# Two pairs of VectorE sums merged into one each, with negative copies from ScalarE

## The chip, the cores and the metric

The kernel runs on one core of a Trainium2 chip. The metric is the device time of one execution in microseconds, the median of several runs. Engines are called as in the profile: PE (TensorE, with PEld for its weight loads), DVE (VectorE), ACT (ScalarE), POOL (GpSimd), SP (SyncE, which issues most DMAs here).

## What is computed

The reference has three stages, all on 2 series of 12480 tokens with 128 channels:

```
u      = x * v
h      = (relu(pos_emb @ w1) @ w2) * exp(-0.01 * pos)
y      = irfft(rfft(u, 2S) * rfft(h, 2S))[:S]        # a long causal convolution, per channel
t      = x * y                                        # 24960 tokens x 128
t      = (g * cos(g)) @ w_out,   g = t @ w_in         # d_ff = 2048
out    = (g * min(max(g+3,0),6) / 6) @ w_out2,  g = t @ w_in2
```

## The kernel before

The convolution is done in place of a longer FFT as a product of two cyclic transforms on a grid of 111 x 113 points (12543 points), with a sign pattern `sig` for the second (odd) half. Channels go in groups of two (`CH = 2`, `NG = 64` groups), each with both series. One group passes four stages, which different rounds of one loop work on: `s1` (first transform along 111, on PE, 4 products in a group of columns `g`: 0 and 1 for the two series, 2 for the filter), `s2h` and `s2u` (second transform along 113 of the filter `xh` and of the signal `xp`), then on DVE `mk_pq` and `mk_y` (product of the spectra), `s2i` (back along 113), `s1i` (back along 111, giving `v1` and `v2` in PSUM), and `mk_w` (DVE), `fin` (POOL) and `store` (SP).

The loop `for i in range(NG)` at line 536 is written out by hand, in program order for every engine: in round `i` it issues, in this order, the loads for group i+3, the stores of group i-4, `s1(i+1, 2)`, `s2i(i-2, 0)`, `s1(i+1, 0)`, `s2i(i-2, 1)`, `s1(i+1, 1)`, `make_p(i+2)`, in odd rounds `copy_h`, `make_q`, `sums_h`, `s2h(i)`, `mk_w(i-3)`, one step of the two weight decoders (`step_decode`, lines 114 to 139: some rounds have three ACT instructions of it, some none), `make_u(i+2)`, `fin(i-3)`, `s2u(i)`, `s1i(i-2)`, `mk_pq(i)`, `mk_y(i)`. Each engine takes its own instructions in that order, so an instruction that waits holds all behind it on its engine.

What PE writes goes to PSUM, and is brought to SBUF by ACT: `at` (line 298, from `ap`), `b` (line 470, from `bp`), `hs` (line 422, from `xh`), `v2s` (line 480, from `v2`). PSUM buffers: `ps_a` has two, which `s1(.,2)`, `s2i(.,0)`, `s2i(.,1)` and `s1(.,1)` take in turn; `ps_c` has one, for `s1(.,0)` and `s2h`; `ps_v` one, for `v1` and `v2` in two banks. A PSUM buffer is free again when its last reader is through.

The product of the spectra: `xp` holds real and imaginary part of the signal (z = 0, 1), `hs` those of the filter. `mk_pq` makes `p = xp * hs_re` in SBUF and then overwrites `xp` (in PSUM) with `q = xp * hs_im`; both are 896 elements wide. `mk_y` writes `y_re = p_re - q_im` and `y_im = p_im + q_re`, two instructions of 448 elements. `mk_w` writes `w = v1 + v2` and `w = v1 - v2` into the two halves of each row, two instructions of 456 elements:

```
for z, op in ((0, ALU.subtract), (1, ALU.add)):             # mk_y, line 451
    nc.vector.tensor_tensor(out=y[..z half..], in0=p[:, z], in1=q[:, 1 - z], op=op)
for h, op in ((0, ALU.add), (M2, ALU.subtract)):            # mk_w, line 485
    nc.vector.tensor_tensor(out=o[:, :, h:h + M2], in0=v1_t[i], in1=v2_t[i], op=op)
```

After the loop (lines 572 to 635) the last groups are finished in halves by series; those use `mk_pq` and `mk_y` with a series number `b`, but their own `w_of` in place of `mk_w`. A DMA at line 619 reads back from `scr` the first 448 tokens of all earlier groups (it can only start when their stores have landed), `pass_on` sends the last groups' ones straight to `x0`, and `split_x(0)` (line 671: `x0h` on ACT, `x0l` on DVE) opens the two expert stages, `moe_phase`, which take the rest of the time.

Of the kernel before, what the change touches and what calls it, by code (L numbers as in the profile page):

```python
# [9 lines left out]
FP32 = mybir.dt.float32  # L10
# [3 lines left out]
ACTF = mybir.ActivationFunctionType  # L14
ALU = mybir.AluOpType
# [6 lines left out]
B, S, D = 2, 12480, 128  # L22
R = 64
N1, N2 = 111, 113
N = N1 * N2
NP1 = 112
K1 = 56
M2 = 57
# [21 lines left out]
def kernel(  # L50
# [19 lines left out]
    nc = tc.nc  # L70
# [90 lines left out]
    def conv_phase(cctx):  # L161
# [30 lines left out]
        p_2 = cctx.enter_context(tc.tile_pool(name="p_2", bufs=2))  # L192
# [5 lines left out]
        x_t, v_t, a_t, hs_t, xp_t, pq_t, y_t, b_t, v1_t, v2_t, w_t, wa_t, z_t = ({} for _ in range(13))  # L198
# [82 lines left out]
        def mm(out, lhsT, rhs, rhs2=None):  # L281
            m = lhsT.shape[-1]
            nc.tensor.matmul(out=out[:OD], lhsT=lhsT[:, :OD], rhs=rhs)  # L283
            nc.tensor.matmul(out=out[OD:m], lhsT=lhsT[:, OD:m], rhs=rhs if rhs2 is None else rhs2)  # L284
# [123 lines left out]
        p_1 = cctx.enter_context(tc.tile_pool(name="p_1", bufs=1))  # L408
# [5 lines left out]
        def s2_mm(o, q0, q1, a):  # L414
            for z in range(2):
                mm(o[z], cs[:, z, :], a[:, z, q0:q1, :])

        def s2h(i):
            ap = ps_c.tile([N2, 2, 4, K1], FP32, tag="a", name="xh")
            s2_mm((ap[:, 0], ap[:, 1]), 8, 12, a_t[i])  # L420
            hs = p_2.tile([N2, 2, 4 * K1], FP32, tag="hs", name="hs")
            nc.scalar.copy(hs, ap.rearrange("p z s k -> p z (s k)"))
            hs_t[i] = hs

        def s2u(i):
# [5 lines left out]
        def mk_pq(i, b=None):  # L431
            if i not in pq_t:
                xv = xp_t.pop(i)[:, :, :448].rearrange("p z (b k) -> p z b k", b=B)
                pq_t[i] = (p_1.tile([N2, 2, B, 4 * K1], FP32, tag="pq", name="pq"), xv)
            p, xv = pq_t[i]
            hs = hs_t[i]
            for z, o in ((0, p), (1, xv)):
                if b is None:
                    h = hs[:, z, :].unsqueeze(1).unsqueeze(1).to_broadcast([N2, 2, B, 4 * K1])
                    nc.vector.tensor_tensor(out=o, in0=xv, in1=h, op=ALU.mult)  # L440
                else:
                    h = hs[:, z, :].unsqueeze(1).to_broadcast([N2, 2, 4 * K1])
                    nc.vector.tensor_tensor(out=o[:, :, b], in0=xv[:, :, b], in1=h, op=ALU.mult)

        def mk_y(i, b=None):
            p, q = pq_t[i]
            if i not in y_t:
                y_t[i] = p_2.tile([N2, 8, 2 * K1], FP32, tag="y", name="y")
            bs = slice(0, B) if b is None else slice(b, b + 1)
            y = y_t[i][:, 4 * bs.start:4 * bs.stop]  # L450
            for z, op in ((0, ALU.subtract), (1, ALU.add)):
                nc.vector.tensor_tensor(
                    out=y[:, :, z * K1:(z + 1) * K1],
                    in0=p[:, z, bs].rearrange("p b (s k) -> p (b s) k", k=K1),
                    in1=q[:, 1 - z, bs].rearrange("p b (s k) -> p (b s) k", k=K1), op=op,
                )

        def s2i(i, g, pool=None):
            if not 0 <= i < NG:
# [12 lines left out]
        def s1i(i):  # L472
            b = b_t.pop(i)
            v = ps_v.tile([NP1, 2, 512], FP32, tag="v", name="v")
            v1, v2 = [v[:, z, :8 * M2].rearrange("p (a b) -> p a b", b=M2) for z in range(2)]
            for z, o in ((1, v2), (0, v1)):
                mm(o, gm[:, z, :], b[:, :, z * M2:(z + 1) * M2])
            v1_t[i] = v1
            v2_t[i] = p_1.tile([NP1, 8, M2], FP32, tag="v2s", name="v2s")
            nc.scalar.copy(v2_t[i], v2)  # L480

        def mk_w(i):
            w = w_t[i] = p_2.tile([NP1, B, 2, CH, MP], FP32, tag="w", name="w")
            o = w.rearrange("p b s c n -> p (b s c) n")
            for h, op in ((0, ALU.add), (M2, ALU.subtract)):
                nc.vector.tensor_tensor(out=o[:, :, h:h + M2], in0=v1_t[i], in1=v2_t[i], op=op)

        def fin(i):
            z = z_t[i] = p_2.tile([NP1, B, CH, MP], FP32, tag="z", name="z")
# [46 lines left out]
        for i in range(NG):  # L536
# [15 lines left out]
            if i:  # L552
                make_q(i + 2)
            sums_h((i + 3) // 2, (1,) if i and i % 2 == 0 else (0,))
            s2h(i)
            if i >= 3:
                mk_w(i - 3)
# [9 lines left out]
            if i >= 2:  # L567
                s1i(i - 2)
            mk_pq(i)
            mk_y(i)  # L570

        n = NG
# [29 lines left out]
        s1i_3(0)  # L602
        s2i(n - 2, 0)
        mk_pq(n - 1, 0)
        mk_y(n - 1, 0)
        s2i(n - 1, 0)
        s1i_of(n - 2, 0, ps_c, "a")
        s1i_of(n - 1, 0, ps_p, "p")
        w_of(n - 3, 0, w3[:, 0])
        fin_of(n - 3, 0, z3[:, 0], nc.gpsimd)  # L610
        mk_pq(n - 1, 1)
        mk_y(n - 1, 1)
        w_of(n - 2, 0, w2_[:, 0])
        fin_of(n - 2, 0, z2[:, 0], nc.gpsimd)
# [342 lines left out]
```

## Time and profile before

| | us |
|---|---|
| median of 3 runs (2617.3 to 2620.01) | 2617.63 |
| the profiled execution | 2617.47 |
| its span in the profile | 2615.7 |

| busy in the span | us | share | instructions |
|---|---|---|---|
| PE | 2598.3 | 99% | 16362 |
| DVE | 2344.5 | 90% | 3188 |
| ACT | 2150.5 | 82% | 3140 |
| POOL | 2394.7 | 92% | 1321 |

The filter is made in the first 38 us, the loop runs from about 38 to 520 us, the last groups are finished by about 535 us, and the expert stages fill the rest. Busy shares over the whole span mix these, so the loop is read by itself. In a timeline each row is one instruction (or several merged, xN), with its start and its length; two instructions in a row on one engine can overlap, so what an instruction costs its engine is the step from its start to the next one's start. Idle time and what ended it stand in square brackets.

### The profile page before, as it was taken

The numbers are of one execution on the slowest core, as the hardware profiler recorded it, in microseconds if no ns is written. First come the engines' busy times: TensorE is split into PE (matmuls) and PEld (weight loads), VectorE is DVE, ScalarE is ACT, GpSimd is POOL, SyncE is SP. The second block draws the span as 40 slices with busy tenths as digits, with TensorE's granted clock in tenths as the row PEclk, the third lists the DMA queues.
The fourth block names the chain that finished last, engine by engine and source line by source line (L and its number), as shares of the span: only waits on it lengthen the run. The fifth ranks groups of instructions, "written<-read, shape, count | busy, mean of one in ns | idle before, by whom it ended". The sixth has DMA issues, their size and how long they took to land.

```text
span 2615.7 us, 45720 instructions
## 1 busy us (share of the span) xinstructions
PE 2598.3 (99%) x16362; PEld 2149.6 (82%) x16362; DVE 2344.5 (90%) x3188; ACT 2150.5 (82%) x3140; POOL 2394.7 (92%) x1321
## 2 busy tenths in 40 slices
PE   9999999989999999999999999999999999999999
PEld 6777777768888888888888888888888888888888
DVE  7999998779999999999999999999999999999997
ACT  5666665588888888888888888888888888888885
POOL 6999999788999999999999999999999999999998
PEclk9999999999999999999999999999999999999999
DMA  4433433210000000000000000000000000000000
GB/s 120 108 102 100 104 105 83 67 33 8 17 9 17 9 17 9 17 9 17 17 9 17 9 17 9 17 9 17 9 16 17 9 17 9 17 9 17 9 9 13
DMA packets 88312, 79.86 MB, mean 31 GB/s; under 512 B 57028, under 2 KB 78870, under 8 KB 88086
## 3 DMA queue, kind: packets, MB, share of 16 engines
q1 hardware_dynamic: 87790, 76.80, 10.9%
q8 instruction: 132, 2.16, 0.3%
q14 instruction: 94, 0.77, 0.1%
q10 hardware_dynamic: 296, 0.13, 0.0%
HBM read 51.15 MB, written 25.74 MB: 29 GB/s over the span
## 4 chain that ended last, share of the span: by engine, by line
PE 97%; ACT 1%; POOL 1%; DVE 1%; DMA 1%; issue 0%; DVEq 0%; POOLq 0%; ACTq 0%; SPq 0%
PE acc L784 39%; PE hb L715 20%; PE ha L715 19%; PE ap L284 5%; PE v L284 4%; PE xp L284 3%; PE bp L284 3%; PE xh L284 2%; PE ap L283 1%; PE rp L336 1%; PE hps L349 0%; PE bp L283 0%; DMA x<-scr 0%; POOL lo L749 0%; ACT r L736 0%
## 5 line engine op out<-in xcount | busy, mean ns | idle before, releaser
L774 POOL TENSOR_TENSOR lo<-g,hi 128x1024 fp32r<-128x1024 f32 (+1 forms) x390 | 938.7, 2407 | 141.3 <-DVE hi L771 131.9
L749 POOL TENSOR_TENSOR lo<-g,hi 128x1024 fp32r<-128x1024 f32 (+1 forms) x392 | 941.2, 2401 | 2.4 <-ACT hi L744 1.9
L726 ACT ACTIVATE k<-ha,biasq 128x512 int32<-128x512 f32 (+1 forms) x768 | 494.6, 687 | 214.0 <-PE ha L715 208.5
L737 DVE TENSOR_TENSOR g<-ha,r 128x512 f32<-128x512 f32 (+1 forms) x768 | 500.0, 690 | 171.9 <-ACT r L736 171.7
L715 PE MATMUL hb<-x2h,vi 128*128 128x512 f32 (+1 forms) x1564 | 530.5, 379 | 0.0
L736 ACT ACTIVATE r<-r,biaspi 128x512 f32<-128x512 f32 (+1 forms) x776 | 520.8, 720 | 9.6 <-DVE r L727 7.7
L715 PE MATMUL ha<-xh,wi 128*128 128x512 f32 (+1 forms) x1524 | 519.5, 381 | 3.5 <-DVE g L737 3.5
L727 DVE SCALAR_TENSOR_TENSOR r<-k,ha 128x512 f32<-128x512 int32 (+1 forms) x768 | 489.8, 679 | 3.1 <-ACT k L726 2.8
L757 DVE SCALAR_TENSOR_TENSOR g<-q,hb 128x1024 f32<-128x1024 f32 (+1 forms) x391 | 473.1, 1210 | 7.0 <-ACT q L756 5.5
L771 DVE SCALAR_TENSOR_TENSOR hi<-q,hb 128x1024 fp32r<-128x1024 f32 (+1 forms) x390 | 470.4, 1206 | 0.0
L756 ACT ACTIVATE q<-hb,bias 128x1024 f32<-128x1024 f32 (+1 forms) x391 | 429.9, 1100 | 18.0 <-PE hb L715 17.4
L784 PE MATMUL acc<-hi,wo 128*128 128x512 f32 (+1 forms) x1568 | 406.7, 379 | 0.0
L784 PE MATMUL acc<-hi,vo 128*128 128x512 f32 (+1 forms) x1568 | 406.4, 379 | 0.0
L744 ACT CAST hi<-g 128x1024 fp32r<-128x1024 f32 (+1 forms) x385 | 399.3, 1037 | 0.0
L784 PEld LDWEIGHTS acc<-hi,wo 128*128 128x128 f32 x1568 | 294.8, 188 | 50.1
L784 PEld LDWEIGHTS acc<-hi,vo 128*128 128x128 f32 x1568 | 294.3, 188 | 49.3
L715 PEld LDWEIGHTS hb<-x2h,vi 128*128 128x128 f32 x1564 | 293.5, 188 | 50.1 <-issue 0.8
L715 PEld LDWEIGHTS ha<-xh,wi 128*128 128x128 f32 x1524 | 286.4, 188 | 56.9 <-issue 3.0
L715 PE MATMUL hb<-x2l,vi 128*128 128x512 f32 (+1 forms) x782 | 296.5, 379 | 0.0
L715 PE MATMUL ha<-xl,wi 128*128 128x512 f32 (+1 forms) x762 | 290.3, 381 | 0.0
L784 PE MATMUL acc<-lo,wo 128*128 128x512 f32 (+1 forms) x784 | 235.0, 380 | 1.0 <-POOL lo L749 1.0
L784 PE MATMUL acc<-lo,vo 128*128 128x512 f32 (+1 forms) x784 | 235.1, 380 | 0.0
(155 smaller groups left out, 4081.5 us busy)
## 6 DMA issues: line engine op xcount, KB each, us to landing
x<-in_x_dram SPq DMA_DIRECT2D x64, 199.5 KB
v<-in_v_dram SPq DMA_DIRECT2D x64, 199.5 KB
scr<-z SPq DMA_DIRECT2D x128, 98.9 KB
out_dram<-o SPq DMA_DIRECT2D x47, 256.0 KB
xf<-scr SPq DMA_DIRECT2D x17, 256.0 KB
wst<-in_wi_dram SPq DMA_DIRECT2D x8, 512.0 KB
wst<-in_wo_dram SPq DMA_DIRECT2D x8, 512.0 KB
pt<-in_post_dram SPq DMA_DIRECT2D x14, 224.0 KB
```

Source lines behind the costliest of these rows:

```text
L284: nc.tensor.matmul(out=out[OD:m], lhsT=lhsT[:, OD:m], rhs=rhs if rhs2 is None else rhs2)
L715: nc.tensor.matmul(out=given(hs[c][:, 0, :n]), lhsT=w["i", e][:, sl], rhs=taken(r[:, :n]), start=(k == 0), stop=(k == 2),)
L726: nc.scalar.activation(out=k[:, c, :n], in_=h, func=ACTF.Identity, bias=biasq, scale=1.0 / TWO_PI)
L727: nc.vector.scalar_tensor_tensor(out=un.r[:, c, :n], in0=k[:, c, :n], scalar=-TWO_PI, in1=h, op0=ALU.mult, op1=ALU.add)
L736: nc.scalar.activation(out=rc, in_=rc, func=ACTF.Sin, bias=biaspi, scale=1.0)
L737: nc.vector.tensor_tensor(out=un.g[:, c, :n], in0=h, in1=rc, op=ALU.mult)
L749: nc.gpsimd.tensor_tensor(out=un.lo[:, :, :n], in0=un.g[:, :, :n], in1=un.hi[:, :, :n], op=ALU.subtract)
L756: nc.scalar.activation(out=un.r[:, c, :n], in_=h, func=ACTF.Relu, bias=bias3, scale=1.0)
L757: nc.vector.scalar_tensor_tensor(out=un.g[:, c, :n], in0=un.r[:, c, :n], scalar=6.0, in1=h, op0=ALU.min, op1=ALU.mult)
L771: nc.vector.scalar_tensor_tensor(out=un.hi[:, c, :n], in0=un.r[:, c, :n], scalar=6.0, in1=h, op0=ALU.min, op1=ALU.mult)
L774: nc.gpsimd.tensor_tensor(out=un.lo[:, :, :n], in0=un.g[:, :, :n], in1=un.hi[:, :, :n], op=ALU.subtract)
L784: nc.tensor.matmul(out=given(acc[e][:, :n]), lhsT=w["o", e][:, sl], rhs=taken(r[:, c, :n]), start=(u == 0 and c == 0 and k == 0), stop=(u ...
```

## The change

`hs` gets a third part, a negative copy of the imaginary part, made by a second ACT instruction from the same PSUM tile, and has one buffer in place of two. `mk_pq` takes the parts (im, -im) as they stand in `hs[:, 1:3]` for the second product, so that `q` is (re * im_h, -(im * im_h)). `mk_y` is then one sum over 896 elements, with the two parts of `q` read in reverse order. `v2s` gets a second half, `-v2`, made by a second ACT instruction, and `mk_w` is one sum over 912 elements, with `v1` read twice. Rounds with `mk_y`: 63, and two halves after the loop; with `mk_w`: 61.

```diff
--- before.py
+++ after.py
@@ -418,8 +418,11 @@
         def s2h(i):
             ap = ps_c.tile([N2, 2, 4, K1], FP32, tag="a", name="xh")
             s2_mm((ap[:, 0], ap[:, 1]), 8, 12, a_t[i])
-            hs = p_2.tile([N2, 2, 4 * K1], FP32, tag="hs", name="hs")
-            nc.scalar.copy(hs, ap.rearrange("p z s k -> p z (s k)"))
+            hs = p_2.tile([N2, 3, 4 * K1], FP32, tag="hs", name="hs", bufs=1)
+            nc.scalar.copy(hs[:, :2], ap.rearrange("p z s k -> p z (s k)"))
+            nc.scalar.activation(
+                out=hs[:, 2], in_=ap[:, 1].rearrange("p s k -> p (s k)"), func=ACTF.Copy, scale=-1.0
+            )
             hs_t[i] = hs
 
         def s2u(i):
@@ -434,12 +437,11 @@
                 pq_t[i] = (p_1.tile([N2, 2, B, 4 * K1], FP32, tag="pq", name="pq"), xv)
             p, xv = pq_t[i]
             hs = hs_t[i]
-            for z, o in ((0, p), (1, xv)):
+            for h, o in ((hs[:, :1].to_broadcast([N2, 2, 4 * K1]), p), (hs[:, 1:3], xv)):
                 if b is None:
-                    h = hs[:, z, :].unsqueeze(1).unsqueeze(1).to_broadcast([N2, 2, B, 4 * K1])
+                    h = h.unsqueeze(2).to_broadcast([N2, 2, B, 4 * K1])
                     nc.vector.tensor_tensor(out=o, in0=xv, in1=h, op=ALU.mult)
                 else:
-                    h = hs[:, z, :].unsqueeze(1).to_broadcast([N2, 2, 4 * K1])
                     nc.vector.tensor_tensor(out=o[:, :, b], in0=xv[:, :, b], in1=h, op=ALU.mult)
 
         def mk_y(i, b=None):
@@ -448,12 +450,11 @@
                 y_t[i] = p_2.tile([N2, 8, 2 * K1], FP32, tag="y", name="y")
             bs = slice(0, B) if b is None else slice(b, b + 1)
             y = y_t[i][:, 4 * bs.start:4 * bs.stop]
-            for z, op in ((0, ALU.subtract), (1, ALU.add)):
-                nc.vector.tensor_tensor(
-                    out=y[:, :, z * K1:(z + 1) * K1],
-                    in0=p[:, z, bs].rearrange("p b (s k) -> p (b s) k", k=K1),
-                    in1=q[:, 1 - z, bs].rearrange("p b (s k) -> p (b s) k", k=K1), op=op,
-                )
+            nc.vector.tensor_tensor(
+                out=y.rearrange("p q (z k) -> p z q k", z=2),
+                in0=p[:, :, bs].rearrange("p z b (s k) -> p z (b s) k", k=K1),
+                in1=q[:, ::-1, bs].rearrange("p z b (s k) -> p z (b s) k", k=K1), op=ALU.add,
+            )
 
         def s2i(i, g, pool=None):
             if not 0 <= i < NG:
@@ -476,14 +477,16 @@
             for z, o in ((1, v2), (0, v1)):
                 mm(o, gm[:, z, :], b[:, :, z * M2:(z + 1) * M2])
             v1_t[i] = v1
-            v2_t[i] = p_1.tile([NP1, 8, M2], FP32, tag="v2s", name="v2s")
-            nc.scalar.copy(v2_t[i], v2)
+            v2_t[i] = p_1.tile([NP1, 2, 8, M2], FP32, tag="v2s", name="v2s")
+            nc.scalar.copy(v2_t[i][:, 0], v2)
+            nc.scalar.activation(out=v2_t[i][:, 1], in_=v2, func=ACTF.Copy, scale=-1.0)
 
         def mk_w(i):
             w = w_t[i] = p_2.tile([NP1, B, 2, CH, MP], FP32, tag="w", name="w")
-            o = w.rearrange("p b s c n -> p (b s c) n")
-            for h, op in ((0, ALU.add), (M2, ALU.subtract)):
-                nc.vector.tensor_tensor(out=o[:, :, h:h + M2], in0=v1_t[i], in1=v2_t[i], op=op)
+            nc.vector.tensor_tensor(
+                out=w.rearrange("p b s c (h n) -> p h (b s c) n", h=2),
+                in0=v1_t[i].unsqueeze(1).to_broadcast([NP1, 2, 8, M2]), in1=v2_t[i], op=ALU.add,
+            )
 
         def fin(i):
             z = z_t[i] = p_2.tile([NP1, B, CH, MP], FP32, tag="z", name="z")
```

## Rows read from the trace of the kernel before

**Rows 1.** windows view, 60 us inside the loop; columns engine busy (x instructions), granted clock, DMA share, GB/s
```profile
300.00:360.00 60.00, 60.00 (x824) 44.16 (x822) 54.34 (x91) 39.34 (x77) 57.45 (x56) 1.00 0.40 107
```

**Rows 2.** chain of waits, first matmul of `v` in rounds 2 and 62; start, us, what
```profile
54.90 0.39 PE v L284
...
516.11 0.38 PE v L284
```

**Rows 3.** waits from 60 to 480 us; who for whom: total us, times, longest us
```profile
PEld v L284 <- issue: 51.9, 220, 0.2
...
DVE p L238 <- ACT p L230: 34.2, 40, 1.3
```

**Rows 4.** timeline of DVE in one round; start us, us, engine, line, operation
```profile
301.84 1.08 DVE L440 TENSOR_TENSOR pq<-xp,hs 113x896 f32<-113x896 f32 x1
302.84 1.09 DVE L440 TENSOR_TENSOR xp<-xp,hs 113x896 f32<-113x896 f32 x1
303.97 1.15 DVE L452 TENSOR_TENSOR y<-pq,xp 113x448 f32<-113x448 f32 x2
305.04 1.17 DVE L486 TENSOR_TENSOR w<-v,v2s 112x456 f32<-112x456 f32 x2
306.12 0.42 DVE L137 TENSOR_SCALAR wex<-wex 128x512 int32<-128x512 int32 x1
```

**Rows 5.** timeline of ACT in a round with weight decoding
```profile
306.79 0.36 ACT L230 COPY p<-x 111x228 f32<-111x228 f32 x1
...
307.55 0.54 ACT L422 COPY hs<-xh 113x448 f32<-113x448 f32 x1
307.97 0.73 ACT L124 ACTIVATE wex<-wex,b_exp 128x512 int32<-128x512 int32 x1
...
309.36 0.61 ACT L126 ACTIVATE wmh<-wmh 128x512 f32<-128x512 int32 x1
310.18 0.54 ACT L480 COPY v2s<-v 112x456 f32<-112x456 f32 x1 [0.20 <-PE v L284]
310.97 0.53 ACT L298 COPY at<-ap 121x448 f32<-121x448 f32 x1 [0.26 <-PE ap L283]
```

**Rows 6.** timeline of PE in the same round
```profile
308.39 0.55 PE L284 MATMUL v<-b,gm 112*48 112x456 f32 x1
...
309.95 0.26 PE L284 MATMUL ap<-f,hf 111*57 111x112 f32 x1
...
312.27 0.26 PE L284 MATMUL bp<-f,y 113*48 113x114 f32 x1
```

**Rows 7.** chain of waits behind the loop
```profile
520.66 1.08 POOL z L492
...
524.23 2.08 DMA scr<-z
...
526.38 6.59 DMA x<-scr
```

**Rows 8.** timeline of DVE in the last round
```profile
518.35 1.15 DVE L452 TENSOR_TENSOR y<-pq,xp 113x448 f32<-113x448 f32 x2
519.42 1.17 DVE L486 TENSOR_TENSOR w<-v,v2s 112x456 f32<-112x456 f32 x2
```

**Rows 9.** timeline of ACT at the start of the expert stages
```profile
534.16 0.56 ACT L680 CAST x0h<-x 128x448 fp32r<-128x448 f32 x1 [1.75 <-DMA x<-z]
```

**Rows 10.** timeline of DVE in round 0
```profile
44.15 1.09 DVE L440 TENSOR_TENSOR xp<-xp,hs 113x896 f32<-113x896 f32 x1
45.28 1.15 DVE L452 TENSOR_TENSOR y<-pq,xp 113x448 f32<-113x448 f32 x2
...
46.68 1.23 DVE L122 TENSOR_SCALAR wmh<-wst 128x512 int32<-128x512 int32 x1
```

**Rows 11.** timeline of POOL in round 0
```profile
46.52 1.10 POOL L246 TENSOR_TENSOR hf<-hh 111x456 f32<-111x456 f32 x1 [2.04 <-issue]
```

**Rows 12.** timeline of ACT in round 1
```profile
46.29 0.54 ACT L422 COPY hs<-xh 113x448 f32<-113x448 f32 x1
```

## The prediction

> **What bounds the kernel now.** The page's table of slices shows PE nearly full everywhere; that says little, since a busy PE need not be PE at its peak. So I went to the windows view inside the loop, the only long stretch that the change touches: in 60 us of it PE is busy 60.00 at a granted clock of 1.00, DVE 54.34, POOL 57.45, ACT 39.34 [rows 1]. Three engines are near full, and which one sets the round must be told by waits. In the chain of waits the first matmul of `v` comes at 54.90 us in round 2 and at 516.11 in round 62: 461.21 / 60 = 7.687 us a round [rows 2]; between these the chain holds PE rows and nothing else. The list of waits from 60 to 480 us says the same from the other side: PE's weight loads have gaps of at most 0.2 us each, put down to issue, 220 for 55 rounds, four in a round, so part of the normal rhythm of the four passes of `v`; no such wait on DVE or ACT has any size. DVE on the other hand waits for ACT's copy `p`, 34.2 us in 40 pieces [rows 3]. DVE thus has spare time: 60 - 54.34 = 5.66 us in 60 / 7.687 = 7.8 rounds, 0.73 us a round [rows 1]. The loop is bound by PE, which the change leaves alone. What can move is where PE takes over from others: before it is in stride (rounds 0 to 2), behind the loop, and at any hand-over within the round whose slack the new ACT work uses up.
>
> **DVE, per round.** The pair for `y` holds DVE from 303.97 to 305.04, 1.07 us; the pair for `w` from 305.04 to 306.12, 1.08; one instruction of 896 elements (`pq` to `xp`) from 301.84 to 302.84, 1.00 [rows 4]. So the merged `y` (896) should hold it 1.00, the merged `w` (912) 1.00 + 16/896 = 1.02: 0.07 + 0.06 = 0.13 us saved a round. The sum of the lengths of two instructions is not the price: neighbours overlap. The bounds for a merged one: from 1.00 to twice that, should the engine read `q`'s parts backwards, or `v1` over again, at half pace; no row shows either pattern. Nearest is `mk_pq`, which reads `hs` over again with a stride of zero at 1.00, so I take 1.00. In the loop the 0.13 is worth nothing, for DVE waits already; it adds to its 0.73 us of spare time.
> [...]
>
> **ACT, per round.** Two instructions come in: the negative `hs` (113x224) and the negative `v2s` (112x456). Nearest in size are the copy of 111x228 at 0.36 us, and `v2s` itself at 0.54; the dearest ACT instruction of about that width is a decoder's at 0.73 [rows 5]. From start to start the step behind `hs` is 0.42 (307.55 to 307.97), so the lengths overstate. I take 0.36 + 0.54 = 0.90 with no overlap, and 0.73 + 0.73 = 1.46 as the upper end. ACT is busy 39.34 x 7.687 / 60 = 5.04 us a round [rows 1], so there is room on the average. Where it could hurt is one place: both new instructions stand ahead of the copy `at` of `s1(i+1, 2)`, whose PSUM buffer (one of `ps_a`'s two) PE needs again for `s2i(i-2, 1)`. The worst round is one with three decoder instructions, where ACT runs without a pause from `hs` on: `v2s` starts at 310.18 after 0.20 idle, `at` at 310.97 after 0.26 idle, and ends at 311.50; PE's next use of the buffer is 312.27 [rows 5, 6]. Slack: 0.20 + 0.26 + 0.77 = 1.23 us. By 0.90 `at` ends 0.90 - 0.46 = 0.44 late, at 311.94, 0.33 before PE asks; with overlap earlier still. The copies behind it come a third of 2.32 apart, 0.77 (three groups from 309.95 to 312.27), and last 0.54, so ACT has caught up by the third. Cost: nothing, hidden by PE's 2.3 us between the two uses of the buffer (309.95 to 312.27). In rounds without decoding ACT is idle ahead of `v2s`, and only the second copy counts.
>
> **The other new orders.** Each one has slack, so they go together. `mk_pq` needs the negative `hs`: `hs` starts at 307.55, both are done by 308.5 on these prices, and `mk_pq` of that round runs after `s2u`, not before 308.39 when PE turns to `v`. `mk_w` needs the negative `v2s`: due by 311.4, used a round after 305.04, so at about 312.7. `ps_v`: ACT reads `v2` one instruction longer, but it is `mk_w`, later still, that frees the bank, 306.2 against PE's 308.39 [rows 4, 6]. The one buffer of `hs`: the next `hs` must wait for the last `mk_pq`. That ends at 303.93 and the next `hs` starts at 307.55, 3.6 us later [rows 4, 5]. Tightest is the start: DVE is through with `hs` of round 0 at 45.24, ACT starts the next one at 46.29 [rows 10, 12]: 1.05 us. In no round does it hold anything. SP's and POOL's queues keep their order, and the merged sums have, as before, one operand in PSUM and one in SBUF.
>
> **Behind the loop.** Here DVE is on the path. POOL's `fin` of group 60 starts at 520.66 when `w` is done, its stores take until 526.31, then `x<-scr` starts at 526.38 and takes 6.59 us [rows 7]. `mk_w(60)` stands on DVE behind `mk_y(62)`: the pair `y` starts at 518.35, `w` at 519.42 and ends at 520.59 [rows 8]. Merged, `y` gives 0.07, and `w` ends after 1.08 + 0.02 = 1.10 in place of 1.17, another 0.07: 0.14 us earlier. `x0h` starts at 534.16, released by one of the small `x<-z` transfers that queue up around that read [rows 9]; their group comes through `mk_y(63)` in halves, which gain about as much each. I carry on 0.1 of the 0.14, with 0 and 0.14 as bounds.
>
> **The start.** `y` of round 0 is on the chain, at 45.28; merged it would give 0.07. But the decoder's instruction at 46.68 is 1.23 us long, and ends when POOL's `hf` (46.52 to 47.62) has [rows 10, 11], so I count 0, with -0.07 as the bound.
>
> **Sum.** Loop 0, end -0.1, start 0: 2617.47 - 0.1 = 2617.4 us by the profiled execution (span 2615.7 and 1.8 around it), which is 0.16 below the median of the runs shown, 2617.63. [...] The bounds of the terms make 2617.3 to 2617.5; the runs themselves lie between 2617.3 and 2620.01, so the likeliest case reaches from 2616 to 2620.5. Under 0.2% (5.2 us) a measurement of this kernel can't tell a change from none.
>
> **Rivals.** *The loop was DVE's after all*: if PE's even rhythm only follows DVE, 0.13 us a round comes back, 62 x 0.13 = 8 us: 2609.4. For it: DVE and POOL are over 90% busy in the loop [rows 1]. Against it: DVE waits 34 us for ACT and PE for no one [rows 3]. Chance 0.03. [...]
> *ACT late with `at`*: the place and the slack of 1.23 us are named above; it decides only if the two negative copies together hold ACT longer than that. At 1.46 PE would wait 0.23 in each round with three decoder instructions; there are 16 decoding tasks, so 16 x 0.23 = 4 us: 2621. For it: the copies are ACTIVATEs and the kernel's dearest such row is 0.73 [rows 5]. Against it: that one writes integers over 512 columns, and the one on 512 with a mere factor takes 0.61 [rows 5]. Chance 0.05; by the bound above it would still count as no change.
> *Slower: DVE reads the new patterns at half pace.* Place: the merged `y`, whose reversed operand lies in PSUM, and `w`, which reads `v1` twice. From 0.73 us more a round (the spare time), less the gain, DVE becomes the round. With `y` alone at 2.00 it is 1.00 - 0.13 = 0.87 over, so 0.14 x 62 = 9 us: 2626; with both, 1.00 + 1.02 - 0.13 = 1.89 over, 1.16 x 62 = 72 us: 2689. Against it: `pq` and `xp` read a zero stride at full pace, and `y` has runs of 56 elements in either form. Chance 0.05.
> *The change doesn't do what it says*: merged instructions hold DVE as long as a pair. That is the forecast's time plus 0.1, and counts with it.
>
> **How the numbers follow.** Forecast 0.87, ACT late 0.05, half pace 0.05, loop bound by DVE 0.03. Faster by over 0.2%: 0.03, and 0.01 for a luckier hand-over to the expert stages, 0.04. Slower: 0.05, and 0.01 from the ACT case at its worst, 0.06. Within 0.2%: 0.90. Time 2617.4. The range takes in the scatter of the runs and the ACT case: 2615.5 to 2621.
>
> **What would show it.** Right: in the loop PE still 60.00 of 60 and 7.687 us a round; DVE's step behind `y` and `w` about 1.00 each, its busy time per 60 us lower by about 1 and its wait for `p` longer; ACT up by some 6 us per 60; `at` in decoding rounds starting up to 0.4 us later with PE not waiting; POOL's `z` of group 60 some 0.1 us earlier against the last matmul of `xp`. Wrong: a round other than 7.687 us, PE waiting for ACT's `at` or for `uf`, a merged instruction well over 1.1 us, or ACT idle before `hs` for want of its one buffer.

## The result, and the profile after

The changed kernel takes 2641.09 us (median of 4 runs, 2640.36 to 2641.34), the kernel before beside it 2617.47 (4 runs, 2616.86 to 2620.01): a ratio of 1.0088, 95% interval 1.0076 to 1.01. Forecast were 2617.4 us and "no change" at 0.90; the time lies outside the range. The profiled span grew from 2615.7 to 2639.1, by 23.4 us.

Where the 23.4 us lie can be read from `w`, the step that both kernels run 61 times. Timeline of DVE after, first and last `w` in the loop:

```profile
57.89 1.10 DVE L486 TENSOR_TENSOR w<-v,v2s 112x912 f32<-112x912 f32 x1
...
542.04 1.10 DVE L486 TENSOR_TENSOR w<-v,v2s 112x912 f32<-112x912 f32 x1
```

First `w` before:

```profile
58.60 1.17 DVE L486 TENSOR_TENSOR w<-v,v2s 112x456 f32<-112x456 f32 x2
```

Before, the last starts at 519.42 [rows 8], 460.82 us behind the first; after, it is 484.15. That is +23.33. The start is 0.71 earlier, and from the last `w` to the end of the span it is 2096.3 before and 2097.1 after. So the loop lost it. Windows view after (columns as in [rows 1]), two stretches with weight decoding and one behind it:

```profile
300.00:360.00 60.00, 57.30 (x793) 48.49 (x791) 50.56 (x71) 41.01 (x87) 57.97 (x50) 1.00 0.39 102
360.00:420.00 60.00, 56.70 (x748) 48.23 (x746) 48.47 (x70) 39.23 (x84) 57.86 (x50) 0.97 0.34 91
450.00:510.00 60.00, 60.00 (x806) 51.25 (x804) 48.03 (x65) 36.98 (x82) 51.60 (x56) 1.00 0.30 83
```

PE has fallen from 60.00 busy to about 57, and POOL is still at 58, with fewer instructions (50 where [rows 1] has 56). DVE is down from 54.34 [rows 1] to 50.56 in the same stretch, so it isn't the bound. DVE's last decoder instruction ends at 444.53 us, and behind it PE is back at 60.00: the loss belongs to rounds with decoding. Waits after, from 60 to 500 us (total, times, longest):

```profile
DVE uf L243 <- POOL q L222: 40.1, 35, 2.9
DVE p L238 <- ACT p L230: 29.8, 36, 1.9
...
PE ap L284 <- POOL hf L246: 15.4, 11, 1.8
```

The first was 2.9 us before and the third did not occur: now DVE waits for POOL's `q`, PE for POOL's `hf`. One round shows it. DVE after:

```profile
309.13 1.09 DVE L453 TENSOR_TENSOR y<-pq,xp 113x896 f32<-113x896 f32 x1
310.14 1.10 DVE L486 TENSOR_TENSOR w<-v,v2s 112x912 f32<-112x912 f32 x1
311.16 0.68 DVE L133 SCALAR_TENSOR_TENSOR wmh<-wst,wmh 128x512 f32<-128x512 uint32 x1
311.75 0.42 DVE L121 TENSOR_SCALAR wex<-wst 128x512 int32<-128x512 int32 x1
312.09 0.42 DVE L122 TENSOR_SCALAR wmh<-wst 128x512 int32<-128x512 int32 x1
...
316.13 1.17 DVE L243 TENSOR_TENSOR uf<-p,q 111x456 f32<-111x456 f32 x2 [2.66 <-POOL q L222]
...
320.34 1.10 DVE L486 TENSOR_TENSOR w<-v,v2s 112x912 f32<-112x912 f32 x1
```

POOL in the same stretch:

```profile
309.20 1.07 POOL L495 TENSOR_TENSOR z<-w,sig 112x456 f32<-112x456 f32 x1
310.35 3.17 POOL L496 TENSOR_TENSOR z<-z,w 112x456 f32<-112x456 f32 x1
313.60 1.15 POOL L497 TENSOR_TENSOR z<-z,x 112x456 f32<-112x456 f32 x1
314.71 0.67 POOL L219 TENSOR_TENSOR q<-x,v 111x228 f32<-111x228 f32 x1
315.46 0.63 POOL L222 TENSOR_TENSOR q<-q,sig 111x228 f32<-111x228 f32 x1
316.05 1.00 POOL L246 TENSOR_TENSOR hf<-hh 111x456 f32<-111x456 f32 x1
...
320.53 1.78 POOL L219 TENSOR_TENSOR q<-x,v 111x228 f32<-111x228 f32 x1
```

And PE, where `hf` is wanted:

```profile
315.25 0.36 PE L283 MATMUL ap<-f,hf 111*64 111x112 f32 x2
317.10 0.30 PE L284 MATMUL ap<-f,hf 111*57 111x112 f32 x1 [1.50 <-POOL hf L246]
```

The row to look at is POOL's 3.17 us. It waits for nothing in the records, yet the same line takes 1.16 in other rounds. It starts while DVE works on `w`, and ends 1.01 us behind the end of the third decoder instruction (312.51): of its 1.16 us of work all but 0.15 came after the decoder. So POOL stood still while the decoder's instructions ran on DVE, and it stood already while `w` was in front of them. All behind it on POOL comes 2 us late: `q`, hence `uf` on DVE, and `hf`, hence PE.

From here on, the excess of a row is what it is longer than the shortest of its line and shape in the same trace, and a POOL instruction is called held when its excess is over 0.1 us. The sum of the excess of all POOL rows that start from 60 to 450 us is called POOL's stretch, and the same sum over DVE's decoder instructions (lines 121, 122, 128, 133, 137) DVE's stretch. POOL's stretch is 42.1 us before and 70.4 after. A POOL instruction counts as begun during a DVE instruction when it starts more than 0.03 us behind that one's start and more than 0.03 us ahead of the next one's. In the changed kernel all 47 that began during a `w` with a decoder instruction behind it were held; in the kernel before, all 40 that began during the second instruction of the `w` pair. In 418 of the 419 such held rows of all traces here the excess is the time from POOL's own start to the end of the decoder instruction (of the last one, where several follow each other), less 0.11 to 0.15 us: POOL stands from its start until the decoder is through.

The trace of before had it too, between rows that I had read. DVE before:

```profile
312.41 1.17 DVE L486 TENSOR_TENSOR w<-v,v2s 112x456 f32<-112x456 f32 x2
313.49 0.68 DVE L128 SCALAR_TENSOR_TENSOR wex<-wst,wex 128x512 int32<-128x512 int32 x1
```

POOL before:

```profile
312.61 0.68 POOL L219 TENSOR_TENSOR q<-x,v 111x228 f32<-111x228 f32 x1
313.37 1.30 POOL L222 TENSOR_TENSOR q<-q,sig 111x228 f32<-111x228 f32 x1
```

`L219` began in the first `w` and was left alone; `L222` began in the second, 0.12 ahead of the decoder, and took 1.30 in place of 0.64. In the merged kernel the instruction ahead of the decoder is 1.02 us from start to start in place of 0.54, so the stretch of time in which POOL must not begin anything is twice as long.

The round feeds itself. POOL's `q` releases `uf`, and behind it DVE goes through `pq`, `xp` and `y` to the next `w`, 4.21 us later (316.13 to 320.34). POOL turned to `hf` and the three `z` at the same moment, and its next start falls 0.19 us behind the start of `w`, at 320.53: held again, 1.78 in place of 0.68. Taken from one `w` to the next, decoding rounds now last 6.9 to 10.2 us, where nearly all before are 7.69 or pairs of 8.0 and 7.4 that make up for each other. Behind the decoding `w` holds nobody. DVE after:

```profile
458.00 1.10 DVE L486 TENSOR_TENSOR w<-v,v2s 112x912 f32<-112x912 f32 x1
```

POOL after:

```profile
457.16 1.16 POOL L496 TENSOR_TENSOR z<-z,w 112x456 f32<-112x456 f32 x1
458.41 1.16 POOL L497 TENSOR_TENSOR z<-z,x 112x456 f32<-112x456 f32 x1
```

Here `w` runs from 458.00 to 459.10 with no decoder instruction behind it; `L497` began inside it and has its usual length.

From 60 to 430 us PE is busy 370.0 us of 370 before and 355.2 after, 14.8 idle. The granted clock of windows of 60 us was 1.00 before; after it is 0.97 in three of them (120:180, 240:300, 360:420). In each of these there are 3.4 us (from 169.8, 268.8 and 367.8) at 0.50, and each begins within 1.3 us of the end of a wait of PE for `hf` of 1.8 us. In the chain of waits one step of `bp` takes 0.19 us there (from 170.24 to 170.43) in place of 0.10 (169.50 to 169.60). As an estimate from these figures the clock of 0.50 costs half of 3 x 3.4 = 5.1 us, 19.9 together. From 430 to 446 us PE is busy 16.00 of 16, so the other 3.4 us are not there; they stay unplaced.

### The profile page after: what moved, and what is told of

Same layout as the page of the kernel before. It is cut to its first block, busy times and chain, and to the rows that moved or that the text cites. A ratio compares the mean times of both kernels' runs of the same rounds, so it can differ in the third digit from the quotient of the medians.

```text
span 2639.1 us, 45840 instructions
## 1 busy us (share of the span) xinstructions
PE 2605.8 (99%) x16362; PEld 2203.1 (83%) x16362; DVE 2336.6 (89%) x3062; ACT 2188.6 (83%) x3265; POOL 2421.8 (92%) x1321
## 4 chain that ended last, share of the span: by engine, by line
PE 89%; POOL 8%; ACT 1%; DVE 1%; issue 1%; DMA 0%; POOLq 0%; ACTq 0%; DVEq 0%
PE acc L787 39%; PE hb L718 20%; PE ha L718 19%; PE ap L284 3%; PE bp L284 2%; POOL z L497 2%; POOL z L496 2%; POOL hf L246 1%; PE xp L284 1%; PE v L284 1%; PE xh L284 1%; POOL z L495 1%; PE xp L283 1%; PE v L283 1%; POOL q L219 1%; POOL q L222 1%
```

## The experiments

The theory from the first comparison: *POOL is held by the decoder's DVE instructions, from the start of whatever stands directly ahead of them*. The expectations call it "held port"; port, queue and sequencer in them are guesses at the cause, which no run shows: the rows show who stands, from when and for how long. Rivals: the loss comes from ACT's copies, or from the merged `y`. Later rounds set rivals on what "ahead" depends on: its length, its wait, its operands, its partitions. The kernel before ran beside each group: 2617.75 us (e1 to e4, and again e5 to e8), 2617.64 (e9, e10), 2617.45 (e11, e12), 2618.1 (e13, e14).

| run | median us | ratio (95%) | stretch of POOL / DVE, us | POOL instructions begun during the one ahead |
|---|---|---|---|---|
| before | 2617.47 | | 42.1 / 0.1 | 40 of 40 held |
| after | 2641.09 | 1.0088 (1.0076 to 1.01) | 70.4 / 1.2 | 47 of 47 held |
| e1 | 2617.85 | 0.9999 (0.999 to 1.0009) | 40.2 / 5.2 | 39 held |
| e2 | 2643.3 | 1.0097 (1.0082 to 1.0112) | 73.2 / 0.4 | 47 held |
| e3 | 2618.01 | 1.0 (0.999 to 1.0009) | 41.5 / 0.2 | 40 held |
| e4 | 2617.49 | 1.0 (0.999 to 1.0009) | 15.1 / 27.4 | none began |
| e5 | 2617.81 | 1.0 (0.999 to 1.0009) | 26.7 / 17.1 | 11 held |
| e6 | 2617.14 | 0.9997 (0.9987 to 1.0006) | 42.1 / 6.0 | 40 held |
| e7 | 2625.96 | 1.0031 (1.0019 to 1.0043) | 14.3 / 23.5 | 68, none held |
| e8 | 2621.09 | 1.0013 (1.0003 to 1.0022) | 33.9 / 8.9 | 23 held |
| e9 | 2624.0 | 1.0026 (1.0014 to 1.0037) | 52.2 / 0.5 | 42 held |
| e10 | 2616.64 | 0.9997 (0.9988 to 1.0006) | 23.6 / 24.1 | 47, none held |
| e11 | 2640.98 | 1.0089 (1.0074 to 1.0104) | 70.6 / 0.2 | 47 held |
| e12 | 2616.63 | 1.0001 (0.9991 to 1.001) | 22.1 / 24.6 | 47, none held |
| e13 | 2626.96 | 1.0022 (0.999 to 1.0053) | 57.1 / 4.5 | 43 held |
| e14 | 2617.43 | 0.9991 (0.9954 to 1.0027) | 14.5 / 30.2 | 43, none held |

**Which part.** e1 keeps only the part of `y` (`w` is the pair again), e2 only the part of `w`, e3 only ACT's copies, with both pairs as before.

> Only the product's part of the change: negative copy of hs, merged y; w as the pair of before. Theory (held port): POOL's next instruction is held from the start of the DVE instruction that stands directly ahead of a decoder's SBUF-only instruction; here that is again the second half of w, 0.62 us, so the loop stays at 7.69 us a round and the time at 2616 to 2619 us. Rival (ACT's copies delay the round): about a third of the new ACT work is here, so some 8 us of the 23.5 come back, 2625. Rival (the merged w takes the port by itself, by its pattern): 2617.

> Only w's part of the change: negative copy of v2s, merged w; the product as before. Held port: all of the loss, 2639 to 2643 us, with POOL's instructions behind the start of w stretched by 1.1 to 2.1 us as in the changed kernel. ACT's copies: two thirds of the loss, 2633. Merged w by itself: 2641.

> ACT makes both negative copies, with the tile shapes and the one buffer of hs of the change, but nobody reads them: DVE sums in pairs as before. Held port: 2616 to 2619 us. ACT's copies: all of the loss, 2641. Merged w by itself: 2617.

The merged `w` alone costs it all (+25.6 us); the merged `y` (e1) and the copies (e3) cost nothing that the intervals show.

**A short instruction between.** e4 is the whole change and one more DVE instruction behind `w`:

```diff
+            nc.vector.tensor_tensor(out=gap, in0=v1_t[i][:, 0, :1], in1=v2_t[i][:, 0, 0, :1], op=ALU.add)
```

> The whole change, and one more DVE instruction of 112x1 (one operand in PSUM, one in SBUF) directly behind the merged w, so that a short one stands ahead of the decoder's. Held port: an added instruction wins all back, 2616 to 2619 us, and POOL is stretched no more than before the change (under 0.8 us a round). ACT's copies: 2641. Merged w by itself: 2641, POOL stretched as in the changed kernel.

DVE of e4:

```profile
312.86 1.10 DVE L488 TENSOR_TENSOR w<-v,v2s 112x912 f32<-112x912 f32 x1
313.88 0.15 DVE L492 TENSOR_TENSOR gap<-v,v2s 112x1 f32<-112x1 f32 x1
313.95 1.19 DVE L128 SCALAR_TENSOR_TENSOR wex<-wst,wex 128x512 int32<-128x512 int32 x1
```

POOL of e4:

```profile
312.99 0.64 POOL L222 TENSOR_TENSOR q<-q,sig 111x228 f32<-111x228 f32 x1
313.59 1.00 POOL L246 TENSOR_TENSOR hf<-hh 111x456 f32<-111x456 f32 x1
```

With 0.07 us of another instruction between, both POOL rows that begin during `w` keep their length, and it is the decoder's instruction that waits (1.19 in place of 0.68). One instruction more, and 24 us less than the changed kernel: the loss is the hold, not the work. POOL's and DVE's stretch together are 42 to 48 us in every kernel here at 2616.6 to 2618.0 us, and 70.8 to 73.6 in the changed kernel, e2 and e11: in e4 much of the standing (27.4 us) lies on DVE, which has time to spare (busy 353.5 us of 370 from 60 to 430).

**Length and place.** e5 and e6 split the merged `w` unevenly, 684 and 228 elements or 228 and 684 (`for a, e in ((0, 6), (6, 8))`, or `((0, 2), (2, 8))`). e7 moves `step_decode()` ahead of `mk_w`, so that `y` is directly ahead of it; e8 moves it behind the first part of `make_u`.

> The whole change, but w in two instructions, 684 elements and then 228, so that 0.39 us stand ahead of the decoder's instruction in place of 1.10. Held port: 2616 to 2619 us. If any split won it back, the next kernel, with the same two pieces in the other order, would be as fast.

> The same two pieces of w, 228 elements first and 684 last: 0.86 us ahead of the decoder's. Held port, with the length as its measure: 0.86 is half way from 0.62 (before, 0.77 us a round of stretched POOL) to 1.10 (1.36), so about 1.06 us a round, 0.29 over before; POOL had 2.4 of 60 us spare, some 0.3 a round, so 2618 to 2630, likeliest 2624. If only the number of instructions mattered: 2617.

> The whole change, with the decoders' step issued ahead of mk_w: now the merged y (1.09 us) stands ahead of the decoder's instruction and the merged w behind it. Held port: as slow as the changed kernel, 2636 to 2646 us, though w is out of the way. If it were something in w: 2617.

> The whole change, with the decoders' step issued behind the first part of make_u: an instruction of 0.40 us stands ahead of the decoder's. Held port: 2616 to 2619 us, with POOL stretched less than in the kernel before.

e5 came as expected; e6 was a miss, and so were e7 and, less, e8. In e6 the long instruction ahead held 40, as many as the short one before: the time doesn't go by the length alone. As I read it, it goes by whether POOL's next start falls into the instruction ahead, and POOL's place in the round shifts along; no run here sets that place by itself. e6's own rival, that only the number of instructions matters, had 2617 and so came true here; it falls with e14 below, which has one merged `w` and no loss. e7 was the miss that taught most: behind `y` nothing was held at all, 0 of 68. Its 8.2 us must be another loss; by the waits it is `w`, now late behind the decoder. Waits of e7:

```profile
POOL z L495 <- DVE w L486: 12.6, 15, 1.4
...
PE v L283 <- DVE w L486: 5.7, 15, 0.6
```

In e8 the instruction ahead is `p<-p,sig` (111 partitions), and its 23 were held. POOL's stretch is less than before, as expected (33.9); where e8's 3.3 us come from is not shown.

**Why not behind `y`?** First idea: the decoder's instruction reaches ahead only past an instruction that has to wait for nothing (by my guess `w` is queued up; `y` waits: it starts 1.13 us behind `xp`, where `xp` starts 1.00 behind `pq` [rows 4]). e9 lets a 112x1 instruction ahead of `w` do the waiting; e10 is the change with `mk_w(i - 2)` placed between `mk_pq(i)` and `mk_y(i)`, so that `y`, with no other wait than for DVE itself, is directly ahead.

> The whole change, and an instruction of 112x1 directly ahead of the merged w, which w has to wait for (it writes one element of v2s again, with its own value). The merged w still stands directly ahead of the decoder's instruction, at 1.10 us. Refined theory: the decoder's instruction takes the port early only if it is in DVE's queue by the time the one ahead of it starts; here DVE's sequencer stands at w's wait until w can start, so POOL is not held during w, and the time is 2616 to 2620 us in spite of more DVE work. If the length of the instruction ahead decides alone: 2641. If the merged w holds POOL by itself: 2641.

> The whole change with DVE's order pq, xp, w, y, decoder in place of pq, xp, y, w, decoder: now the merged y, without a wait just before it, stands ahead of the decoder's instruction. Refined theory: POOL instructions that begin while y runs are held until the decoder's is through, as in the changed kernel, and the time is 2630 to 2645 us. If it is the merged w's own pattern: nobody held during y, 2617 to 2620 us.

Both spoke against the idea: in e9 `w` held 42 though it no longer waited, in e10 `y` held none of 47. e9's time, 2624.0, lies between its two forecasts. DVE of e10:

```profile
173.90 1.08 DVE L453 TENSOR_TENSOR y<-pq,xp 113x896 f32<-113x896 f32 x1
174.90 1.84 DVE L128 SCALAR_TENSOR_TENSOR wex<-wst,wex 128x512 int32<-128x512 int32 x1
```

POOL of e10:

```profile
174.52 0.64 POOL L222 TENSOR_TENSOR q<-q,sig 111x228 f32<-111x228 f32 x1
175.11 1.00 POOL L246 TENSOR_TENSOR hf<-hh 111x456 f32<-111x456 f32 x1
```

POOL's row inside `y` has its usual length, and the decoder's takes 1.84 in place of 0.68. Second idea: the side on which the SBUF operand stands (`w` has it second, `y` first). e11 is the change with `w`'s operands exchanged, e12 is e10 with `y`'s.

> The whole change with the operands of the merged w exchanged: in0 is v2s (SBUF), in1 is v1 (PSUM), as y has p and q. Same sum, same length, same order, the decoder's instruction directly behind it. Theory of the operand's side: the instruction ahead hands POOL's hold forward only if its SBUF operand is the second one; now POOL instructions that begin during w run at their normal length, the decoder's instruction waits for POOL instead, and the time is 2615 to 2619 us. If length or queue alone decides: 2641, POOL held from w's start.

> The order of the run before (w ahead of y, decoder's instruction behind y), with the operands of the merged y exchanged: in0 is q (PSUM), in1 is p (SBUF). Theory of the operand's side: POOL instructions that begin during y are held until the decoder's are through, which none was before the exchange; the time goes up from 2617 to somewhere in 2622 to 2645 us, by how many begin early in y. If something else in w made the hold: 2617, no POOL instruction held during y.

Nothing moved in either: that idea fell as well.

**Partitions.** What was left between `w` and `y`: 112 partitions against 113. e13 is e10 with `y` on 112 (`y`, `p`, `q` and the matmul's operands cut to `[:NP1]`, so one of 113 terms of that sum is left out), e14 the whole change with `v`, `v2s` and `w` on 113:

```diff
-            w = w_t[i] = p_2.tile([NP1, B, 2, CH, MP], FP32, tag="w", name="w")
+            w = w_t[i] = p_2.tile([N2, B, 2, CH, MP], FP32, tag="w", name="w")
...
-                in0=v1_t[i].unsqueeze(1).to_broadcast([NP1, 2, 8, M2]), in1=v2_t[i], op=ALU.add,
+                in0=v1_t[i].unsqueeze(1).to_broadcast([N2, 2, 8, M2]), in1=v2_t[i], op=ALU.add,
```

> As e10 (w ahead of y, decoder's instruction behind y), with the merged y on 112 partitions in place of 113, and s2i with 112 of its 113 rows (one term of the sum is left out). If the count of partitions of the instruction ahead decides (w has 112, y 113): POOL instructions that begin during y are held until the decoder's are through, and the time goes up, 2622 to 2645 us. If the count doesn't matter: 2617, nobody held during y, as in e10.

> The whole change with v, v2s and w on 113 partitions in place of 112 (a column of zeros more in gm; the sums are the same). If the count of partitions decides: POOL instructions that begin during w run at their normal length, and the loss goes, 2615 to 2619 us. If it doesn't: 2641, as the changed kernel.

DVE of e13:

```profile
150.54 1.08 DVE L453 TENSOR_TENSOR y<-pq,xp 112x896 f32<-112x896 f32 x1
151.53 0.68 DVE L128 SCALAR_TENSOR_TENSOR wex<-wst,wex 128x512 int32<-128x512 int32 x1
```

POOL of e13:

```profile
150.84 1.92 POOL L219 TENSOR_TENSOR q<-x,v 111x228 f32<-111x228 f32 x1
```

DVE of e14:

```profile
305.16 1.10 DVE L486 TENSOR_TENSOR w<-v,v2s 113x912 f32<-113x912 f32 x1
306.18 0.96 DVE L137 TENSOR_SCALAR wex<-wex 128x512 int32<-128x512 int32 x1
```

POOL of e14:

```profile
305.19 0.64 POOL L222 TENSOR_TENSOR q<-q,sig 111x228 f32<-111x228 f32 x1
305.78 1.07 POOL L273 TENSOR_TENSOR hh<-h,sig 111x456 f32<-111x456 f32 x1
```

One partition less, and `y` holds 43 of 43 (`q` at 1.92 in place of 0.68); one partition more, and `w` holds none of 43 while the decoder's 0.42 become 0.96. e14 is the change itself with a `w` that does slightly more, and is back at the time of before, 2617.43; from 60 to 430 us PE is busy 370.0 of 370. e13's own time isn't told from no change by its interval, which is wide because runs of the kernel before beside it scattered (2634.6 and 2651.35 among them; e14 has one of 2640.85); there the rows decide: PE busy 363.0 of 370, POOL's stretch 57.1.

No version beats the kernel before: with POOL's hold gone the round is PE's again, and the 0.13 us that DVE saves lie beside it (e4, e10, e12, e14 all within 0.2%).

## Why the prediction was wrong

**The step that failed** is the last sentence of "the other new orders": "SP's and POOL's queues keep their order, and the merged sums have, as before, one operand in PSUM and one in SBUF." Both halves are true, and from them POOL's cost was taken as nothing, with neither bound nor price; its spare time, 2.55 us in 60 or 0.33 a round [rows 1], was not worked out as DVE's was. The runs show a term of +23.3 us in its place: the merged `w` is the instruction directly ahead of the decoder's, is twice as long as the one that stood there, and POOL instructions that begin in it stand until the decoder is through. e2 and e4 show that this is the whole loss, e14 that the hold is its cause.

**What I misread.** POOL's 57.45 us of 60 [rows 1] were taken for work. Of POOL's busy time from 60 to 450 us 42.1 us were stretch, which by the rows above is nearly all time standing still. That the waits view names no other engine as holding POOL was no sign of work: the hold shows there in no row, only as a longer row in the timeline. Lines view before, POOL, 60 to 430 us (busy, mean ns, idle before):

```profile
L222 POOL TENSOR_TENSOR q<-q,sig 111x228 f32<-111x228 f32 x48 | 51.5, 1073 | 3.8
L219 POOL TENSOR_TENSOR q<-x,v 111x228 f32<-111x228 f32 x48 | 44.9, 936 | 0.0
```

The same view after:

```profile
L497 POOL TENSOR_TENSOR z<-z,x 112x456 f32<-112x456 f32 x45 | 70.3, 1562 | 3.5
L496 POOL TENSOR_TENSOR z<-z,w 112x456 f32<-112x456 f32 x45 | 66.3, 1474 | 3.5
```

Means of 1073 and 936 for rows of 0.64 and 0.68 were there to be asked about. After, the stretch sits on the two `z`, whose rows otherwise take 1.16: POOL's place in the round has moved.

A sign stood in "The start" too: a decoder's row of 1.23 us where 0.42 is usual, beside POOL's `hf` [rows 10, 11]. It ends at 47.91, 0.29 behind `hf` and not with it, and I took it for a matter of the start alone, without asking what the same two engines do to each other in the loop.

The row that shows the hold best is POOL's 3.17 above. That DVE and POOL hold each other would have been a rival, and I did not weigh it. Who began first does not settle here who stands: POOL's `L496` began 0.81 us ahead of the decoder's instruction, and yet the decoder keeps its 0.68 and POOL stands. In e4, e10 and e14 POOL also began first, and there it is the decoder that stands (1.19, 1.84 and 0.96 on DVE). In e4, e10, e12 and e14, where the decoder waits, the merged sums cost nothing.

**What was right.** That PE bounds the loop: e4, e10, e12 and e14 have the merged instructions and are at 2617. The DVE steps: `y` 1.01 from start to start (309.13 to 310.14) and `w` 1.02 (310.14 to 311.16), for 1.00 and 1.02. The rivals on half pace and on a change that doesn't do what it says are thereby out. DVE's spare time did not show as a longer wait for `p`: from 60 to 500 us it is 29.8 after and 38.1 before, while the wait for `q` grew to 40.1. ACT's prices were 0.36 and 0.54, measured 0.36 and 0.56; timeline of ACT after:

```profile
308.37 0.56 ACT L482 ACTIVATE v2s<-v 112x456 f32<-112x456 f32 x1
...
312.99 0.36 ACT L423 ACTIVATE hs<-xh 113x224 f32<-113x224 f32 x1
```

PE waited for ACT's `at` once from 38 to 540 us, 0.4 us, and e3, which has both copies unread, takes 2618.01. The loop was not DVE's: e1, e4, e10, e12 and e14 have merged sums, and none of them is faster than the kernel before by its interval.

**Small terms.** The start came 0.7 earlier (PE's first `v` of round 2 at 54.02 against 54.73, both from the timeline), for 0 with a bound of -0.07. That is within what single traces differ by: e9 and e10 go through these rounds with the same instructions as the changed kernel and have this `v` at 54.88 and 54.03. Behind the loop it is +0.8 for -0.1; single runs differ by about as much, so this stays open.

## What to carry to other kernels

An engine that is busy without a wait may be standing still, as POOL was in nearly all of its stretch of 42.1 us: compare each row's length with the shortest of its line before calling its busy share work. Where a GpSimd row is longer beside a VectorE instruction (here 3.17 us for 1.16), look at what stands directly ahead of that instruction as well, since here the hold started there; a short instruction between, another order (`w` ahead of `y`), or one more partition was worth 24 us here. And a saving on an engine that isn't the bound was worth nothing here (0.13 us a round on DVE, with e14 at 2617.43 us), while the new shape of its instructions cost 23.3 us on the one that is.

## What the runs showed of the hardware

- Beside a decoder instruction on DVE (128 partitions, all operands in SBUF) POOL rows grew: 0.64 became 1.30 (before), 0.68 became 1.92 (e13), 1.16 became 3.17 us (after).
- With an instruction of 112 (or, in e8 with 23 held, 111) partitions directly ahead, POOL instructions that began during it were held from their start on and DVE kept its pace; with 113, they ran through and DVE's next one waited (0.42 to 0.96 in e14, 0.68 to 1.84 in e10). The counts: 47 of 47 against 0 of 43 for `w`, 43 of 43 against 0 of 47 for `y`.
- Why the border lies between 112 and 113 is open; no run was made with other counts than 111, 112 and 113. The traces hold one more: a decoder instruction on 128 partitions directly ahead of another. Of 157 POOL instructions that began during the first, 136 had the second one over 0.1 us longer than usual (1.23 for 0.42 in round 0 [rows 10]), so there too DVE mostly waited; but that first one works on SBUF alone, so it is not the same case.
- The order of operands, the length of the instruction ahead and its own wait did not change who was held (e11, e12, e6, e9).
- A PSUM operand read with its two halves in reverse order, and one read twice by a stride of zero, went no slower than `pq` and `xp`: 1.09 us for 896 and 1.10 for 912 elements, where `xp` takes 1.09 for 896 [rows 4].
